# Zero products in tile form and small zero transfers ahead of the first group of a dynamic convolution with a gated output

## The chip, the cores and the metric

The kernel runs on one core of a Trainium2 chip. The metric is the device time of one execution in microseconds (us). TensorE (PE) multiplies matrices, VectorE (DVE) and ScalarE (ACT) work elementwise, GpSimd (POOL) does a few elementwise steps and issues DMAs, and SyncE (SP) only issues DMAs. The DMAs that SP issues form one queue, those of POOL another; both run on the same 16 DMA engines.

## The reference

Eight sequences of 4224 rows and 192 channels. Each row has, for each of 8 heads, 7 weights; a softmax over these 7 weighs the row and the 6 before it. What comes out goes through a causal 5-tap convolution (a sigmoid of it is the gate) and through a product with `w_val`; gate times value is multiplied by `w_out`.

```python
# attention: softmax over the last axis of weight_gen, then
x_unf = x_pad[:, idx, :].reshape(B, S, K, H, group)         # K = 7, H = 8, group = 24
x     = np.einsum('bshk,bskhg->bshg', w, x_unf).reshape(B, S, D)
# gate and output
for k in range(5):
    gate_pre += conv_w[k] * xp[:, k:k + S, :]
out = (1 / (1 + np.exp(-gate_pre))) * (x @ w_val) @ w_out
```

The three weight matrices come as float64 and are turned into float32 on the chip.

## The kernel before

Two sequences make a pair; there are 4 pairs, each cut into 9 groups of 480 rows (the last 384), so 36 groups.

**Softmax.** The class `Softmax` handles a chunk of rows of a pair: the first pair has four chunks (8, 8, 16 and 34 rows to a partition), every later pair two (34 and 32). A chunk is loaded into `wt` by two DMAs on SP, one for each sequence (L262). DVE takes maximum, difference, sum and quotient (L273 to L298), ACT the exponential (L284). ACT then spreads the weights into a banded layout in `zt` (`spread`, L310), twelve rows to a piece, and POOL stores each piece to DRAM in `zd` (`store`, L316).

**Groups.** A group loads its rows of x into `xt` (`load_x`, L391) and the bands into `tb` (`load_t`, L417: sixteen DMAs of 16x4x176 float32 each), all on SP. In `bank` (L439) TensorE multiplies the band by x in tiles of 128x32: 64 products to a group, each of which stands in the trace as two records, so 128 records to a group. ACT copies the four banks out of PSUM (`S`, `B`, `A`; L450 to L457), POOL moves strips between partitions by DMA (L466, L468), ACT and DVE form the gate (L474 to L486), TensorE the value (`val`, L494 to L501) and the output product (`omm`, L522 and L529), ACT copies the result out (L544), and SP stores it (L551). `tb` exists twice (`tb_75` and `tb_76`, used in turn), `xt` three times.

**Ahead of the groups.** DVE zeroes `zero` and the two `zt`; ACT and POOL zero the two `tb`; POOL reorders, loads and converts the weights. `stir(14)` has TensorE form 14 bfloat16 products of 128x128 by 128x368 out of `zero`; nothing reads them.

**Order.** All of it is first entered in a list (`Order.add`: engine, assumed duration, a key, dependencies) and then written out engine by engine by a planner, `Order.run`: at each step it takes the engine that can start earliest, and of the entries open there the one with the smallest key. So an entry added early can change the order of everything behind it. What an engine gets is a fixed sequence, and it works through it in that order; SP too, so that a DMA waiting for its data holds up every DMA behind it. Real waits come from the data alone: a reader of a tile waits for its writer, a writer for earlier readers and writers. Besides, SP's DMAs use eight completion counters in turn, so that a DMA also waits for the eighth before it.

The end of the list of preparations before the change:

```python
    placed = [add("ACT", 0.35, 0.9, f, [conv["v"], wz]) for f in place_weights()]
    add("PE", 2.0, -50, lambda: stir(14), [z0], mode=(0,))
```

Of the kernel before, what the change touches and what calls it, by code (L numbers as in the profile page):

```python
# [7 lines left out]
FP32 = mybir.dt.float32  # L8
U32 = mybir.dt.uint32
I64 = mybir.dt.int64  # L10
BF16 = mybir.dt.bfloat16
# [5 lines left out]
class Order:  # L17
# [13 lines left out]
    def add(self, eng, dur, key, fn, deps=(), mode=None, lag=0.0, bytes=0):  # L31
        o = self.Op()
        o.eng, o.dur, o.key, o.fn, o.mode, o.lag, o.bytes = eng, dur, key, fn, mode, lag, bytes
        o.deps = [d for d in dict.fromkeys(deps) if d is not None]
        o.users, o.ready = [], 0.0
        self.ops.append(o)
        return o
# [47 lines left out]
def tile_dynconv_gated_moe(  # L85
# [9 lines left out]
    nc = tc.nc  # L95
# [5 lines left out]
    P = 128  # L101
    HD = P // 2
    Q = 32
# [18 lines left out]
    PITCH = RUN + CELL // 2  # L122
# [6 lines left out]
    const = ctx.enter_context(tc.tile_pool(name="const", bufs=1))  # L129
    wpool = ctx.enter_context(tc.tile_pool(name="wpool", bufs=2))  # L130
    work = ctx.enter_context(tc.tile_pool(name="work", bufs=2))
    dpool = ctx.enter_context(tc.tile_pool(name="dpool", bufs=1, space=bass.MemoryType.DRAM))
    ps_a = ctx.enter_context(tc.tile_pool(name="ps_a", bufs=3, space=bass.MemoryType.PSUM))
# [9 lines left out]
    wvd = const.tile([P, P], FP32, name="wvd")  # L143
    wvm = const.tile([P, HD], FP32, name="wvm")
    zero = const.tile([P, PITCH], FP32, name="zero")
    NWT = 2 * D + KC
    wf = const.tile([P, 2, NWT], FP32, name="wf")
    un = const.tile([P, 2, NWT], U32, name="un")
    raw_t = const.tile([P, 4 * NWT], FP32, name="raw")
    raw = raw_t.bitcast(U32).rearrange("p (g n t) -> p g n t", g=2, t=2)  # L150
# [14 lines left out]
    add = od.add  # L165
# [52 lines left out]
    def place_weights():  # L218

        units = []  # L220

        def runs(dst, src, q0, q1):

            d = dst.rearrange("p (a c) -> p a c", c=Q)
            return ((d[:, :, 0:C], src[:, C * q0:C * q1].rearrange("p (a c) -> p a c", c=C)),
                    (d[:, :, C:Q], src[:, c6 + HC * q0:c6 + HC * q1].rearrange("p (a c) -> p a c", c=HC)))

        pairs = [*runs(wvm, wf[:, 0, 0:D], 4, NQ)]
        for b in range(2):
            hs = slice(HD * b, HD * b + HD)  # L230
            pairs += runs(wvd[hs, hs], wf[hs, 1, 0:D], 4, NQ)
        pairs += [*runs(wva, wf[:, 0, 0:D], 0, 4), *runs(wvb, wf[:, 1, 0:D], 0, 4)]
        for d, v in pairs:
            units.append(lambda d=d, v=v: nc.scalar.copy(out=d, in_=v))  # L234
        return units
# [129 lines left out]
    rows = {}  # L365
# [184 lines left out]
                          ap=[[2 * D, h], [S * D, 2], [1, 2 * D]])  # L550
            nc.sync.dma_start(out=dst, in_=self.ot[0:h, :, k, :])  # L551

    def stir(n):

        z = zero.bitcast(BF16)
        pa = ps_a.tile([P, 512], FP32, name="pa")
        for _ in range(n):
            nc.tensor.matmul(out=pa[:, 0:2 * PITCH], lhsT=z[:, 0:P], rhs=z, start=True, stop=True)

    def once(eng, dur, key, fn, deps=(), **kw):
        return add(eng, dur, key, fn, deps, **kw)

    z0 = once("DVE", 0.3, -99, lambda: nc.vector.memset(zero, 0.0))
# [4 lines left out]
    front = []  # L570

    def fronts(i):
        for u in range(2):
            nc.gpsimd.dma_start(out=zd[i][u, 0:FRONT, :], in_=zero[0:FRONT, :])

    front = [once("POOL", 1.2, -97.5 + 8 * i, lambda i=i: fronts(i), [z0], lag=2.5, bytes=1) for i in range(2)]
# [17 lines left out]
    conv = {}  # L594
    for name, cs, w, key in (("c", slice(2 * D, NWT), "DVE", 0.3), ("v", slice(0, D), "POOL", 0.5),
                             ("o", slice(D, 2 * D), "POOL", 1.5)):
        a = lw
        for eng, f in convert_weights(cs, "DVE", w):
            dur = 0.2 if name == "c" else 0.6 if eng == "DVE" else 1.5
            a = add(eng, dur, key, lambda f=f, eng=eng: f(engs[eng]), [a])  # L600
        conv[name] = a
    placed = [add("ACT", 0.35, 0.9, f, [conv["v"], wz]) for f in place_weights()]
    add("PE", 2.0, -50, lambda: stir(14), [z0], mode=(0,))

# [11 lines left out]
    for m, gp in enumerate(gr):  # L618
        d = {}
        T.append(d)  # L620
        n, w = gp.n, gp.w
# [11 lines left out]
        last = min(gp.s + NW * gp.step, S)  # L633
# [82 lines left out]
```

## Time and profile before

| | |
|---|---|
| Time, two runs | 642.34 and 643.53 us, median 642.93 |
| Span of the profiled execution, first to last instruction | 638.4 us (4.5 us below the median of the runs) |
| Mean granted TensorE clock | 0.888 |
| Busy: PE, DVE, ACT, POOL | 497.9, 432.8, 343.6, 205.3 us |
| Moved by DMA | 122.19 MB, mean 191 GB/s |

The page has the busy times, the span in 40 slices, the DMA queues, the chain of waits that ended last, and groups of instructions. "PEclk" is the share of full clock that TensorE was granted. The views used below are the timeline (start, duration, engine, line, operation), the table of stretches (busy time of each engine in a stretch, its clock and its DMA share), the chain in order of time, and the table of DMA issues with their time to landing. "SPq" and "POOLq" are the queues of these engines.

### The profile page before, as it was taken

How to read it: one execution, taken by the hardware profiler on the slowest of the kernel's cores; microseconds unless marked ns; L12 is line 12 of the kernel's file. 1: busy time of each engine (PE TensorE's matmuls, PEld its weight loads, DVE VectorE, ACT ScalarE, POOL GpSimd, SP SyncE). 2: the span in 40 equal slices, each digit the busy share in tenths (PEclk: the TensorE clock that was granted, in tenths of full speed). 3: DMA queues.
4: the chain of work that ended last, by engine and by line, in shares of the span. 5: the costliest groups of instructions: out<-in, count | busy, mean ns of one | idle time of the engine just before them, and what ended most of it. 6: DMA issues, size and time to landing. Idle time of an engine off the chain costs nothing.

```text
span 638.4 us, 15889 instructions
## 1 busy us (share of the span) xinstructions
PE 497.9 (78%) x6278; PEld 341.2 (53%) x6278; DVE 432.8 (68%) x488; ACT 343.6 (54%) x533; POOL 205.3 (32%) x380
## 2 busy tenths in 40 slices
PE   2036179859679996997769709999389999999995
PEld 1024156546556665665537506766256667766764
DVE  4646768845867895984765564988656488667780
ACT  6235447635655674764635543586336565665542
POOL 9662132323232332322312230442304422342220
PEclk7567589969898998998888867999789999999999
DMA  6967788878688787687877686786858767777633
GB/s 188 268 128 191 184 230 243 200 193 188 158 225 246 216 211 208 178 256 186 230 181 191 174 200 187 185 201 158 239 122 207 205 173 224 180 193 179 165 81 83
DMA packets 116249, 122.19 MB, mean 191 GB/s; under 512 B 20144, under 2 KB 110348, under 8 KB 113424
## 3 DMA queue, kind: packets, MB, share of 16 engines
q1 hardware_dynamic: 102144, 88.31, 53.3%
q0 software_dynamic: 14032, 32.87, 19.9%
q8 instruction: 50, 0.82, 0.6%
q14 instruction: 23, 0.19, 0.1%
HBM read 63.71 MB, written 51.45 MB: 180 GB/s over the span
## 4 chain that ended last, share of the span: by engine, by line
PE 48%; DMA 26%; SPq 15%; ACT 4%; DVE 3%; issue 3%; POOL 1%; ACTq 0%; DVEq 0%; POOLq 0%
PE pa L439 14%; SPq L417 12%; PE po L522 11%; DMA tb<-zd 11%; PE po L529 6%; PE v L498 6%; DMA wt<-in_weight_gen_dram 5%; DMA zd<-zt 4%; PE v L501 4%; PE v L496 4%; PE v L494 3%; DMA out_dram<-ot 3%; SPq L391 2%; ACT zt L310 1%; DMA A<-S 1%
## 5 line engine op out<-in xcount | busy, mean ns | idle before, releaser
L439 PE MATMUL pa<-tb,xt 128*32 128x122 f32 (+3 forms) x4608 | 156.0, 293 | 119.8 <-DMA tb<-zd 111.6
L439 PEld LDWEIGHTS pa<-tb,xt 128*32 128x32 f32 (+3 forms) x4608 | 141.5, 120 | 134.8 <-issue 64.6
L482 DVE SCALAR_TENSOR_TENSOR aA<-A,wf,aA 128x960 f32<-128x960 f32 (+1 forms) x144 | 171.1, 1188 | 25.1 <-ACT aA L474 23.2
L468 POOL DMA_DIRECT2D B<-S x144 | 74.2, 522 | 281.4 <-ACT B L453 272.4
L482 DVE SCALAR_TENSOR_TENSOR aB<-B,wf,aB 128x480 f32<-128x480 f32 (+1 forms) x144 | 101.1, 702 | 75.8 <-ACT aB L477 74.4
L522 PE MATMUL po<-wf,aA 128*120 128x192 f32 (+1 forms) x576 | 116.4, 347 | 8.3 <-ACT ot L544 3.9
L544 ACT COPY ot<-po 120x768 f32<-120x768 f32 (+1 forms) x72 | 57.8, 803 | 114.3 <-PE po L529 70.3
L522 PEld LDWEIGHTS po<-wf,aA 128*120 128x120 f32 (+1 forms) x576 | 94.3, 191 | 40.3 <-issue 24.8
L466 POOL DMA_DIRECT2D A<-S x144 | 74.6, 524 | 49.3 <-ACT A L450 23.2
L457 ACT COPY S<-pa 64x484 f32<-64x484 f32 (+1 forms) x72 | 39.7, 552 | 67.7 <-PE pa L439 67.2
L529 PE MATMUL po<-wf,aB 64*120 64x192 f32 (+1 forms) x576 | 69.8, 361 | 5.2 <-DVE aB L509 3.5
L498 PE MATMUL v<-A,wva 128*128 128x480 f32 (+1 forms) x144 | 62.7, 558 | 1.4 <-ACT wva L234 1.4
L529 PEld LDWEIGHTS po<-wf,aB 64*120 64x120 f32 (+1 forms) x576 | 47.3, 190 | 21.5 <-issue 14.3
L507 DVE TENSOR_TENSOR aA<-v,aA 128x960 f32<-128x960 f32 (+1 forms) x36 | 40.7, 1130 | 23.0 <-ACT aA L486 15.7
L474 ACT ACTIVATE aA<-A,wf 128x960 f32<-128x960 f32 (+1 forms) x36 | 38.8, 1077 | 24.0 <-DMA A<-S 23.7
L316 POOL DMA_DIRECT2D zd<-zt x50 | 26.8, 540 | 72.3 <-ACT zt L310 59.7
L450 ACT COPY A<-pa 128x484 f32<-128x484 f32 (+1 forms) x72 | 39.8, 553 | 12.2 <-PE pa L439 11.1
L498 PEld LDWEIGHTS v<-A,wva 128*128 128x128 f32 x144 | 27.3, 190 | 31.1 <-issue 26.8
L310 ACT COPY zt<-wt 128x192 f32<-128x192 f32 (+3 forms) x100 | 39.0, 463 | 7.8 <-DVE wt L298 3.9
L486 ACT ACTIVATE aA<-aA 128x960 f32<-128x960 f32 (+1 forms) x36 | 35.3, 980 | 8.3 <-DVE aA L482 8.2
L509 DVE TENSOR_TENSOR aB<-v,aB 128x480 f32<-128x480 f32 (+1 forms) x36 | 23.1, 641 | 24.3 <-ACT aB L486 19.0
L494 PE MATMUL v<-A,wvm 128*64 128x480 f32 (+1 forms) x144 | 38.1, 609 | 0.0
(55 smaller groups left out, 371.3 us busy)
## 6 DMA issues: line engine op xcount, KB each, us to landing
tb<-zd SPq DMA_DIRECT2D x560, 44.0 KB
out_dram<-ot SPq DMA_DIRECT2D x64, 360.0 KB
xt<-in_x_dram SPq DMA_DIRECT2D x56, 384.0 KB
zd<-zt POOLq DMA_DIRECT2D x30, 552.0 KB, 6.8
wt<-in_weight_gen_dram SPq DMA_DIRECT2D x8, 560.0 KB
A<-S POOLq DMA_DIRECT2D x128, 30.2 KB, 3.7
zd<-zt POOLq DMA_DIRECT2D x10, 368.0 KB, 8.0
zd<-zt POOLq DMA_DIRECT2D x8, 460.0 KB, 9.1
```

What stands on the lines that cost most here:

```text
L310: nc.scalar.copy(out=dst, in_=src)
L417: nc.sync.dma_start(out=t[lo:lo + n, u * NW + w0:u * NW + w1, c0:c0 + RUN], in_=src)
L439: nc.tensor.matmul(out=pa[Q * c:Q * c + Q, at:at + n], lhsT=self.xb[0:k, u * NW + j, C * h:C * h + Q], rhs=self.t[0:k, u * NW + j, PAD // ...
L466: nc.gpsimd.dma_start(out=self.A[q:q + n, :, 0:w], in_=self.S[p:p + n, :, 0:w])
L468: nc.gpsimd.dma_start(out=self.B[HD * u + q:HD * u + q + n, 0:w], in_=self.S[p:p + n, u, 0:w])
L482: nc.vector.scalar_tensor_tensor(out=a, in0=src, scalar=cw[:, g, j:j + 1], in1=a, op0=ALU.mult, op1=ALU.add)
L494: nc.tensor.matmul(out=v2[HD * u:HD * u + HD, 0:n], lhsT=wvm, rhs=A[:, u], start=True, stop=False, tile_position=(0, HD * u))
L498: nc.tensor.matmul(out=v01[:, u, 0:n], lhsT=wva, rhs=A[:, u], start=True, stop=False)
L507: nc.vector.tensor_tensor(out=self.aA, in0=self.v01[:, :, 0:n], in1=self.aA, op=ALU.mult)
L522: nc.tensor.matmul(out=po[0:h // 2, u, D * t:D * t + D], lhsT=gA[:, u, k, t], rhs=woa, start=first and t == 0, stop=not first, skip_group_ ...
L529: nc.tensor.matmul(out=po[0:h // 2, u, D * t:D * t + D], lhsT=gB[hs, k, t], rhs=wob[hs], start=first and t == 0, stop=not first, skip_grou ...
L544: nc.scalar.copy(out=self.ot[0:h, :, k, :], in_=self.po[0:h, :, 0:2 * D])
```

## The change

`stir` takes a kind now and forms float32 products in tiles: kinds 5 and 6 form 64 products of 128x32 by 128x122 each, kinds 2, 3 and 4 form 160 products of 64x32 by 64x58 each. The kinds differ in how the moving operand is read (`t` pairs with a stride, or single columns with a stride) and, for kind 4, in the PSUM bank that is written. Seven of them are entered one behind the other: 6, 5, 6, 2, 3, 4, 5. They read a new zero tile `scr` of 128x2048, which DVE writes. Nothing reads what they form.

`lay` is new: four entries on SP, 37 DMAs that carry zeros from `scr` to a new DRAM buffer `zs`, from there to a new tile `scr2`, and from `scr` to `scr2`. Nothing reads `scr2`.

```diff
+    scr = const.tile([P, 2048], FP32, name="scr")
+    big = scr
+    scr2 = const.tile([P, 2048], FP32, name="scr2")
+    zs = dpool.tile([P * 8, 184], FP32, name="zs")
...
-    def stir(n):
-        z = zero.bitcast(BF16)
-        pa = ps_a.tile([P, 512], FP32, name="pa")
-        for _ in range(n):
-            nc.tensor.matmul(out=pa[:, 0:2 * PITCH], lhsT=z[:, 0:P], rhs=z, start=True, stop=True)
+    def stir(kind):
+        w = zero[:, 0:PITCH]
+        bk = [ps_a.tile([P, 512], FP32, name="pa") for _ in range(2)]
...
+        elif kind < 4:
+            for i in range(20):
+                for u in range(2):
+                    for c in range(4):
+                        ps = slice(HD * u, HD * u + HD)
+                        mv = (big[ps, 0:464].rearrange("p (a h t) -> p a h t", h=8, t=2)[:, :, c, :] if kind == 2 else
+                              big[ps, 0:464].rearrange("p (a h) -> p a h", h=8)[:, :, c])
+                        nc.tensor.matmul(out=bk[u][Q * c:Q * c + Q, 64 * (i % 8):64 * (i % 8) + 58], lhsT=w[ps, Q:2 * Q],
+                                         rhs=mv, start=True, stop=True, tile_position=(HD * u, Q * c))
+        elif kind == 4:
...
+        else:
+            for i in range(16):
+                for c in range(4):
+                    mv = (big[:, 0:976].rearrange("p (a h t) -> p a h t", h=8, t=2)[:, :, c, :] if kind == 5 else
+                          big[:, 0:976].rearrange("p (a h) -> p a h", h=8)[:, :, c])
+                    nc.tensor.matmul(out=bk[0][Q * c:Q * c + Q, 128 * (i % 4):128 * (i % 4) + 122], lhsT=w[:, Q:2 * Q],
+                                     rhs=mv, start=True, stop=True, tile_position=(0, Q * c))
+
+    def lay(part):
+        if part == 0:
+            nc.sync.dma_start(out=zs.rearrange("(p r) n -> p (r n)", r=8), in_=scr[:, 0:8 * 184])
+            for n in (56, 112):
+                dst = bass.AP(tensor=zs.tensor, offset=zs.offset, ap=[[184 * 8, P], [184, 8], [1, n]])
+                nc.sync.dma_start(out=dst, in_=scr[:, 0:8 * n].rearrange("p (c n) -> p c n", n=n))
+        elif part == 1:
+            for n, q, c in ((56, P, 16), (112, P, 8)):
+                src = bass.AP(tensor=zs.tensor, offset=zs.offset, ap=[[n, q], [P * n, c], [1, n]])
+                nc.sync.dma_start(out=scr2[0:q, 0:c * n].rearrange("p (c n) -> p c n", n=n), in_=src)
+        else:
+            for r in range(16):
+                src = scr[0:HD, 56 * r:56 * r + 56]
+                if part == 2:
+                    nc.sync.dma_start(out=scr2[r:r + HD + 1:HD, 0:1792].rearrange("p (c n) -> p c n", n=56), in_=src)
+                else:
+                    nc.sync.dma_start(out=scr2[r + 16:r + 17, 0:1792].rearrange("p (c n) -> p c n", n=56), in_=scr[0:Q, 56 * r:56 * r + 56])
...
-    add("PE", 2.0, -50, lambda: stir(14), [z0], mode=(0,))
+    b0 = once("DVE", 1.0, -98.5, lambda: nc.vector.memset(scr, 0.0))
+    last = None
+    for k in (6, 5, 6, 2, 3, 4, 5):
+        last = add("PE", 3.0, -50, lambda k=k: stir(k), [z0, b0, last], mode=(0,))
+    for k in range(4):
+        add("SP", 4.0, -88.5 + 0.1 * k, lambda k=k: lay(k), [b0, *front])
```

How the DMAs stand on SP after the early loads of x, before the change (`wt` is a softmax chunk, `tb` a band; the last figures are the shape, `x16` means sixteen in a row):

```order
L391 DMA xt_81<-in_x_dram 128x3x192
L262 DMA wt<-in_weight_gen_dram 64x1232
L262 DMA wt<-in_weight_gen_dram 64x2240
L262 DMA wt<-in_weight_gen_dram 64x1232
L417 DMA tb_75<-zd_79 16x4x176 x16
L262 DMA wt<-in_weight_gen_dram 64x2240
L417 DMA tb_76<-zd_79 16x4x176 x16
```

and after it, where line numbers are 4 higher up to the old `stir` and 67 higher behind it, and `scr_90` is the tile `scr2`:

```order
L395 DMA xt_81<-in_x_dram 128x3x192
L607 DMA zs<-scr 128x1472
L610 DMA zs<-scr 1024x1x56
L610 DMA zs<-scr 1024x1x112
L614 DMA scr_90<-zs 128x16x56
L614 DMA scr_90<-zs 128x8x112
L619 DMA scr_90<-scr 2x32x56 x16
L621 DMA scr_90<-scr 1x32x56 x16
L266 DMA wt<-in_weight_gen_dram 64x1232
L421 DMA tb_75<-zd_79 16x4x176 x7
L266 DMA wt<-in_weight_gen_dram 64x1232
L421 DMA tb_75<-zd_79 16x4x176 x9
```

All 37 new DMAs stand between the last early load of x and the load of the first pair's third softmax chunk (64x1232). Each of the first five writes or reads what the one before it wrote, and the sixth writes over what the fifth wrote. The two loads of the third chunk, which stood two apart, now have seven loads of `tb` between them, and the two of the fourth chunk (64x2240) stand behind the sixteen of `tb_75` and behind nine of `tb_76`.

On TensorE the last bfloat16 products of zeros stood right ahead of the first group's products of `tb_75`:

```order
L558 MATMUL pa<-zero 128x368
L558 LDWEIGHTS zero
L558 MATMUL pa<-zero 128x368
L439 MATMUL pa<-tb_75,xt_81 32x122 x12
L439 MATMUL pa<-tb_75,xt_81 32x118 x4
```

After the change the sequence begins with 736 products in tiles (the figure behind x counts products; the trace has two records for each):

```order
L600 MATMUL pa<-scr,zero 32x122 x192
L584 MATMUL pa<-scr,zero 32x58 x320
L593 MATMUL pa<-scr,zero 32x58 x160
L600 MATMUL pa<-scr,zero 32x122 x64
L443 MATMUL pa<-tb_75,xt_81 32x122 x12
```

The 14 bfloat16 products are gone, and the first group's product of `tb_75` follows the last product of zeros. The order of the entries behind the start is planned anew too, so that the places of output stores among the loads of `tb` differ in the later groups.

More of the change, by code (lines that the diff above doesn't have):

```diff
@@ L551, in store, with rounds @@
             nc.sync.dma_start(out=dst, in_=self.ot[0:h, :, k, :])
-    def stir(n):
-        z = zero.bitcast(BF16)
-        pa = ps_a.tile([P, 512], FP32, name="pa")
-        for _ in range(n):
-            nc.tensor.matmul(out=pa[:, 0:2 * PITCH], lhsT=z[:, 0:P], rhs=z, start=True, stop=True)
+    def stir(kind):
+        w = zero[:, 0:PITCH]
+        bk = [ps_a.tile([P, 512], FP32, name="pa") for _ in range(2)]
+        def rounds(n, rows, cols, cells):
+            h = P // rows
+            for i in range(n):
+                for u in range(h):
+                    for c in range(4):
+                        ps = slice(rows * u, rows * u + rows)
+                        mv = w[ps, 0:2 * cells * 8].rearrange("p (a h t) -> p a h t", h=8, t=2)[:, :, c, :] if cols else \
+                            w[ps, 0:2 * cells * 8].rearrange("p (a h) -> p a h", h=8)[:, :, c]
+                        nc.tensor.matmul(out=bk[(u + i) % 2 if h == 2 else u % 2][Q * c:Q * c + Q, 64 * (i % 4) + 32 * (u // 2):][:, 0:2 * cells],
+                                         lhsT=w[ps, Q:2 * Q], rhs=mv, start=True, stop=True,
+                                         tile_position=(rows * u, Q * c))
+        if kind < 2:
+            rounds(20, P, kind == 0, 11)
+        elif kind < 4:
[8 more added lines that the diff above has]
+        elif kind == 4:
+            for i in range(20):
+                for u in range(2):
+                    for c in range(4):
+                        ps = slice(HD * u, HD * u + HD)
+                        mv = big[ps, 0:464].rearrange("p (a h t) -> p a h t", h=8, t=2)[:, :, c, :]
+                        d = bk[(c // 2 + u) % 2]
+                        nc.tensor.matmul(out=d[Q * c:Q * c + Q, 64 * (i % 8):64 * (i % 8) + 58], lhsT=w[ps, Q:2 * Q],
+                                         rhs=mv, start=True, stop=True, tile_position=(HD * u, Q * c))
+        else:
+            for i in range(16):
+                for c in range(4):
+                    mv = (big[:, 0:976].rearrange("p (a h t) -> p a h t", h=8, t=2)[:, :, c, :] if kind == 5 else
+                          big[:, 0:976].rearrange("p (a h) -> p a h", h=8)[:, :, c])
+                    nc.tensor.matmul(out=bk[0][Q * c:Q * c + Q, 128 * (i % 4):128 * (i % 4) + 122], lhsT=w[:, Q:2 * Q],
+                                     rhs=mv, start=True, stop=True, tile_position=(0, Q * c))
```

## The prediction

> **What bounds the kernel now.** I read the table of stretches first, to see which stage is thin. Its columns are the stretch, the busy time of PE, PEld, DVE, ACT and POOL, the granted clock, the DMA share and GB/s.
>
> ```profile
> core 0: us, PE busy (x) PEld busy (x) DVE busy (x) ACT busy (x) POOL busy (x), PEclk, DMA share, GB/s
> 16.00:32.00 16.00, 0.00 (x0) 0.00 (x0) 10.44 (x23) 3.37 (x9) 10.09 (x14) 0.50 0.94 270
> 32.00:48.00 16.00, 5.03 (x128) 4.65 (x128) 7.97 (x11) 5.11 (x13) 10.17 (x13) 0.70 0.62 126
> 64.00:80.00 16.00, 2.60 (x48) 2.35 (x52) 12.23 (x15) 7.38 (x13) 2.63 (x5) 0.55 0.77 181
> 200.00:300.00 100.00, 90.19 (x1119) 61.89 (x1119) 76.59 (x83) 59.75 (x89) 29.14 (x57) 0.97 0.78 209
> 300.00:400.00 100.00, 72.29 (x856) 49.26 (x858) 61.66 (x69) 48.47 (x77) 24.16 (x47) 0.81 0.76 194
> ```
>
> PE has nothing to do up to 32 us and little up to 80; later it is busy 72 to 90 us in 100. So the start is a chain of latencies, and what lengthens it moves the whole rest, which is dense. The chain of waits in order of time (start, length, what) shows who holds the start:
>
> ```profile
> 4.25 8.36 DMA wt<-in_weight_gen_dram
> ...
> 24.46 9.16 DMA wt<-in_weight_gen_dram
> ...
> 38.31 5.56 DMA tb<-zd
> ...
> 47.27 3.01 DMA tb<-zd
> 50.37 2.14 PE pa L439 x34
> 52.99 1.73 ACT zt L310 x4
> 55.56 8.92 DMA zd<-zt
> ```
>
> Softmax chunks and bands, all loaded by SP. SP's own timeline at the place of the change (start, length of the stretch, issues):
>
> ```profile
> 14.97 2.54 SPq L391 DMA_DIRECT2D xt<-in_x_dram  x6
> 20.93 4.57 SPq L262 DMA_DIRECT2D wt<-in_weight_gen_dram  x3
> 26.91 10.79 SPq L417 DMA_DIRECT2D tb<-zd  x16
> 37.75 0.47 SPq L262 DMA_DIRECT2D wt<-in_weight_gen_dram  x1
> 38.31 9.85 SPq L417 DMA_DIRECT2D tb<-zd  x16
> ```
>
> SP is free from 17.51 to 20.93 (it waits there for a `wt` buffer) and from 25.50 to 26.91; from then to 48.16 it only issues. The other engines' rows, from the timeline:
>
> ```profile
> 1.46 1.90 DVE L567 MEMSET zt<- 128x2208 f32 x1 [0.41 <-issue]
> 12.71 0.97 DVE L273 TENSOR_REDUCE mx<-wt 128x112 f32<-128x784 f32 x1 [7.05 <-DMA wt<-in_weight_gen_dram]
> 33.65 0.80 DVE L273 TENSOR_REDUCE mx<-wt 128x88 f32<-128x616 f32 x1 [4.53 <-DMA wt<-in_weight_gen_dram]
> 38.98 5.03 PE L439 MATMUL pa<-tb,xt 128*32 128x122 f32 x128 [34.03 <-DMA tb<-zd]
> 50.37 5.24 PE L439 MATMUL pa<-tb,xt 128*32 128x122 f32 x96 [6.36 <-DMA tb<-zd]
> 52.53 0.56 ACT L457 COPY S<-pa 64x484 f32<-64x484 f32 x1 [6.80 <-PE pa L439]
> 77.40 5.48 PE L439 MATMUL pa<-tb,xt 128*32 128x122 f32 x96 [13.98 <-DMA tb<-zd]
> 97.19 0.92 PE L529 MATMUL po<-wf,aB 64*120 64x192 f32 x8
> 98.04 3.75 PE L439 MATMUL pa<-tb,xt 128*32 128x122 f32 x128
> ```
>
> The node that counts is group 1's start at 50.37: ACT's copy of its first bank at 52.53 stands ahead of the spread of the third chunk, its stores land at 64.5, and only then come the bands of group 2.
>
> **The change, part by part.** *DVE* gets a memset of 128x2048: 1.90 x 2048/2208 = 1.76, with the gap of 0.41 some 2.2 us. DVE stood idle for 7.05 us until 12.71, which hides it; the price is nothing, and 2.2 us if that wait were gone.
>
> *The 14 bfloat16 products* went beside idle time; nothing is won.
>
> *The zero products.* 64 float32 products were 128 records: 5.03 us at the low clock of 38.98, 3.75 us at 98.04 where the clock was full, so 29 to 39 ns a record. Kinds 5 and 6 are 512 records, 15 to 20 us. Kinds 2 to 4 are 960 records of a form the trace does not have. Its bounds are the same 29 ns, and the row at 97.19, the one with 64-row tiles and a short stretch: 0.92 us for 8 records of 192 columns, 115 ns, which is three times as many columns. The nearer row is that of the 32-column tiles, and 58 columns are half of its 122; I take 29 to 39 ns, 28 to 37 us. With a start at 3.5 us TensorE ends its zeros at 47 to 61 us. Group 0 cannot start before its bands have come, which is later than that, as the next term says: cost nothing. Nor does a warm array bring anything: group 0 would be done 1.3 us sooner, but group 1 waits for its own bands.
>
> *The 37 DMAs on SP* are the term that counts. SP reaches them at 17.51 and passes the third chunk's loads only behind them. First the five that wait for each other. The prices come from the table of DMA issues (KB each, us to landing) and the row of SP's queue:
>
> ```profile
> zd<-zt POOLq DMA_DIRECT2D x30, 552.0 KB, 6.8
> raw<-wd POOLq DMA_DIRECT2D x2, 192.0 KB, 6.2
> raw<-cd POOLq DMA_DIRECT2D x1, 5.0 KB, 3.8
> zd<-zero POOLq DMA_DIRECT2D x4, 7.2 KB, 2.6
> q1 hardware_dynamic: 102144, 88.31, 53.3%
> ```
>
> From below: a small transfer lands in 2.6 us, and the five carry 736, 224, 448, 448 and 448 KB, 2.36 MB, which at the 270 GB/s of the stretch from 16 to 32 are 8.7 us: 5 x 2.6 + 8.7 = 21.7 us. From above: the queue's mean packet takes 0.533 x 638.4 x 16 / 102144 = 53 ns; the four with short pieces have 1024, 1024, 2048 and 1024 of them, on each of 16 engines 64, 64, 128 and 64, so 3.4, 3.4, 6.8 and 3.4 us, and the first 736 KB at 270 GB/s 2.8: with five times 2.6 that is 32.8 us. The pieces are 224 and 448 bytes where the mean packet has 865, so I take a value near the lower end, 23 us. The Trainium skill ("DMA: Bandwidth & Descriptors", Specifications) gives 512 bytes as the least transfer for full rate and speaks of read-modify-write below it; by that the upper end would be the better guess and the sum some 10 us larger. No packet of the trace shows it apart from others.
>
> Then 32 small ones. SP's issue took 0.47 us by itself (37.75) and 10.79/16 = 0.67 us in the stretch that also waited for earlier loads: 15.0 to 21.6 us; with idle queues the lower, 15. So SP is through at 17.5 + 23 + 15 = 55.5 us, with ends of 54 and 72.
>
> Behind it stand the same four chunk loads and 32 bands as before, in another mixture. Before they took 48.16 - 20.93 = 27.2 us, of which 1.4 was the wait at 25.50 for `zd`, which will long be there, and some waits inside the first three: the bands 10.79 + 9.85, four loads at 0.47 to 0.5, 22.6 us in all. Group 1 started 2.2 us after the last band (50.37 - 48.16). So it starts at 55.5 + 22.6 + 2.2 = 80.3 instead of 50.37: +29.9 us. If every issue took 0.47, 36 of them would take 16.9, and it would be 74.6, +24.2. Group 0 gets its bands at 55.5 + 0.9 + 12.1 (38.98 - 26.91) = 68.5, behind the end of the zeros at 47 to 61.
>
> Is the third chunk ready then? Its second load comes 5.7 us behind SP's return and lands at the 9.16 us of the chain at some 70.4; before, it landed at 33.65 and 19.3 us later its spread began, of which 6 were spent behind the fourth chunk's load, which now stands behind it on DVE. So it is ready at some 84, about when group 1's first bank is copied (80.3 + 2.2 = 82.5). From there the chain is the one of before, shifted by 30 us. Nothing takes it back: DVE, ACT and POOL have done the weights meanwhile, but these were not in the chain.
>
> The profiled span was 638.4 and the median 642.93; I add the difference to both alike: 642.93 + 29.9 = 672.8, rounded to **673 us**.
>
> **The rivals.** *The short transfers run on two engines.* Sixteen of them write 2 partitions each. If one is carried by 2 engines, these have 32 pieces each, at 53 ns 1.7 us for one transfer instead of 0.47 for its issue: 16 x 1.2 = 20 us more, **693 us**. The trace cannot tell, as it shows queues and no engines; for the cheap side speak the half-size pieces. The Trainium skill says just this ("DMA: Bandwidth & Descriptors", Why a DMA increments its semaphore by 16 and not by 1): a transfer uses the largest number of engines up to 16 that divides both outer dimensions. I give it 0.13.
>
> *The 64x32 products do not run beside each other.* At 115 ns a record the 960 take 110 us, the zeros end at 3.5 + 20 + 110 = 134, group 0 waits for them, and group 1 starts at 139: +88, **731 us**. It decides from 54 ns a record (75 us less 3.5 and 20, over 960). Against it: four column tiles at 29 ns for 122 columns. 0.04.
>
> *The new order gives it back: not slower.* SP is held by output stores that wait for ACT while bands stand behind them:
>
> ```profile
> SPq L551 <- ACT ot L544: 40.6, 11, 6.5
> ...
> SPq L417 <- DMA xt<-in_x_dram: 18.0, 17, 2.6
> ```
>
> Eleven waits, 40.6 us, up to 6.5 each. The whole later order is planned anew, so some of them may go; 18 us would go if the stretch from 300 to 400 (72.29 us of PE work) ran like the one from 200 to 300 (90.19). With the shift at its lower 23 us that leaves +5, **648 us**; beyond 36 us regained it would be faster by 2%. It decides from 17 us regained. For it: PE waits are large there. Against it: a new order can as well add such waits. 0.13 for not slower by over 2%, 0.04 for faster.
>
> **How the numbers follow.** Forecast 673 with 0.66 of the chance, two engines 0.13, products apart 0.04, given back 0.13 within 2% and 0.04 below. 2% is 12.9 us, about what a measurement can tell from no change. So faster 0.04, same 0.13, slower 0.83. Range: the cheapest SP term, 54.2 with issues of 0.47, gives +23 and 666; with part of the 18 us of a new order 652. The dearest, 72 + 24.8, gives 97, +46.5 and 689; with two engines on top of the middle 693, to 695. So 652 to 695.
>
> **What would show it.** In the changed kernel's timeline: SP's zero loads from 17.5 to some 55, of which the first five have gaps of 2.5 to 6 us between them; the third chunk's load right behind; group 0 at some 68 and group 1 at some 80; PE's zeros over by 61. Wrong it is if SP is through by 40 us, if group 1 starts before 63, or if the end moves by 10 us less or more than group 1's start, which would put the cause into the later order.

## The result and the profile after

The changed kernel takes 679.36 us (two runs, 677.81 and 680.90), against 642.93 before: the medians differ by 36.4 us, and the ratio is 1.058 with a 95% interval of 1.0495 to 1.0668, which is +37 us (+32 to +43). It is slower, as forecast, and inside the stated range, 6 us above the forecast of 673. The profiled span grew by 40.7 us, from 638.4 to 679.1. Here and below, a ratio leaves out executions that took over 1.5% more than the fastest of their kernel, and the microseconds given with it are the ratio applied to the time before, which can lie some 4 us from the difference of the medians.

The timeline of SP in the changed kernel at the place of the change (start, length of the stretch, line, issues):

```profile
15.02 2.55 SPq L395 DMA_DIRECT2D xt<-in_x_dram  x6
17.67 0.43 SPq L607 DMA_DIRECT2D zs<-scr  x1
26.56 5.99 SPq L610 DMA_DIRECT2D zs<-scr  x2
37.17 5.15 SPq L614 DMA_DIRECT2D scr<-zs  x2
45.72 8.91 SPq L619 DMA_DIRECT2D scr<-scr  x16
54.68 10.09 SPq L621 DMA_DIRECT2D scr<-scr  x16
64.89 0.52 SPq L266 DMA_DIRECT2D wt<-in_weight_gen_dram  x1
65.51 3.34 SPq L421 DMA_DIRECT2D tb<-zd  x7
...
82.25 3.39 SPq L421 DMA_DIRECT2D tb<-zd  x7
```

The third chunk's load, which went out at 20.93, now goes out at 64.89. In between stand the five transfers that wait for each other (17.67 to 45.72, with holes) and the 32 small ones (to 64.77, without a hole). The chain in order of time shows the five landings one behind the other:

```profile
17.67 8.88 DMA zs<-scr
26.56 5.37 DMA zs<-scr
31.99 5.16 DMA zs<-scr
37.17 4.76 DMA scr<-zs
41.95 3.76 DMA scr<-zs
```

TensorE's and ACT's timelines, the rows that answer to those of before:

```profile
3.25 18.09 PE L600 MATMUL pa<-scr,zero 128*32 128x122 f32 x384 [3.25 <-DVE scr L665]
21.27 1.14 PE L584 MATMUL pa<-scr,zero 64*32 64x58 f32 x95
...
52.13 2.87 PE L600 MATMUL pa<-scr,zero 128*32 128x122 f32 x97 [1.17 <-issue]
76.73 5.91 PE L443 MATMUL pa<-tb,xt 128*32 128x122 f32 x128 [21.73 <-DMA tb<-zd]
91.51 4.57 PE L443 MATMUL pa<-tb,xt 128*32 128x122 f32 x96 [8.87 <-DMA tb<-zd]
93.80 0.56 ACT L461 COPY S<-pa 64x484 f32<-64x484 f32 x1 [10.55 <-PE pa L443]
94.26 2.50 ACT L314 COPY zt<-wt 128x192 f32<-128x192 f32 x8
```

The zeros end at 55.0 us, 21.7 us before group 0 has its bands. Group 1 starts at 91.51 instead of 50.37 (+41.1), the third chunk's spread at 94.26 instead of 52.99 (+41.3). The span grew by 40.7. So in these two executions all of it is there before the third group, and nothing is given back or lost in the 580 us behind it.

### The profile page after: what moved, and what is told of

It reads as the page before. It is cut to its first block, busy times and chain, and to the rows that moved or that the text cites. A ratio compares the mean times of both kernels' runs of the same rounds, so it can differ in the third digit from the quotient of the medians.

```text
span 679.1 us, 18853 instructions
## 1 busy us (share of the span) xinstructions
PE 528.6 (78%) x7736; PEld 366.7 (54%) x7736; DVE 434.4 (64%) x489; ACT 343.8 (51%) x533; POOL 204.5 (30%) x380
## 3 DMA queue, kind: packets, MB, share of 16 engines
q0 software_dynamic: 14032, 32.87, 19.1%
## 4 chain that ended last, share of the span: by engine, by line
PE 51%; DMA 24%; SPq 13%; ACT 5%; issue 4%; DVE 1%; POOL 0%; ACTq 0%; DVEq 0%
PE pa L443 15%; PE po L526 13%; SPq L421 8%; DMA out_dram<-ot 7%; PE po L533 7%; PE v L502 6%; DMA tb<-zd 5%; PE v L500 4%; DMA wt<-in_weight_gen_dram 4%; PE v L505 4%; PE v L498 4%; DMA zs<-scr 3%; DMA zd<-zt 2%; ACT zt L314 2%; SPq L621 1%
## 5 line engine op out<-in xcount | busy, mean ns | idle before, releaser
L443 PE MATMUL pa<-tb,xt 128*32 128x122 f32 (+3 forms) x4608 | 150.8, 285 | 88.4 <-DMA tb<-zd 72.2
L443 PEld LDWEIGHTS pa<-tb,xt 128*32 128x32 f32 (+3 forms) x4608 | 135.6, 116 | 105.4 <-issue 88.0
L486 DVE SCALAR_TENSOR_TENSOR aA<-A,wf,aA 128x960 f32<-128x960 f32 (+1 forms) x144 | 170.9, 1187 | 18.4 <-ACT aA L478 14.4
L526 PE MATMUL po<-wf,aA 128*120 128x192 f32 (+1 forms) x576 | 119.6, 353 | 12.7 <-ACT ot L548 8.4
L526 PEld LDWEIGHTS po<-wf,aA 128*120 128x120 f32 (+1 forms) x576 | 96.9, 195 | 44.4 <-issue 21.7
L533 PE MATMUL po<-wf,aB 64*120 64x192 f32 (+1 forms) x576 | 69.6, 362 | 24.2 <-DVE aB L513 23.3
L511 DVE TENSOR_TENSOR aA<-v,aA 128x960 f32<-128x960 f32 (+1 forms) x36 | 40.8, 1132 | 23.6 <-PE v L505 12.5
L478 ACT ACTIVATE aA<-A,wf 128x960 f32<-128x960 f32 (+1 forms) x36 | 38.8, 1077 | 24.9 <-DMA A<-S 22.2
L277 DVE TENSOR_REDUCE mx<-wt 128x160 f32<-128x1120 f32 (+3 forms) x18 | 21.5, 1197 | 45.9 <-DMA wt<-in_weight_gen_dram 45.9
```

The costliest lines, as they stand in the source:

```text
L443: nc.tensor.matmul(out=pa[Q * c:Q * c + Q, at:at + n], lhsT=self.xb[0:k, u * NW + j, C * h:C * h + Q], rhs=self.t[0:k, u * NW + j, PAD // ...
L486: nc.vector.scalar_tensor_tensor(out=a, in0=src, scalar=cw[:, g, j:j + 1], in1=a, op0=ALU.mult, op1=ALU.add)
L511: nc.vector.tensor_tensor(out=self.aA, in0=self.v01[:, :, 0:n], in1=self.aA, op=ALU.mult)
L526: nc.tensor.matmul(out=po[0:h // 2, u, D * t:D * t + D], lhsT=gA[:, u, k, t], rhs=woa, start=first and t == 0, stop=not first, skip_group_ ...
L533: nc.tensor.matmul(out=po[0:h // 2, u, D * t:D * t + D], lhsT=gB[hs, k, t], rhs=wob[hs], start=first and t == 0, stop=not first, skip_grou ...
```

## The experiments

The theory: SP's queue is held for as long as it stands and issues; the third chunk's spread moves by that, and the end moves with the spread. The rivals: the planner's new order makes part of it; the zero products do; the traffic of the transfers does, wherever they stand.

The names: in the kernels whose label begins with o, the rest is in the order of the kernel before, DVE writes the zero tile `scr` right behind `zero`, and the transfers, where there are any, are put by hand in front of the third chunk's load; "n_none" has the changed kernel's order. The cuts of code leave out lines; they show what differs from the changed kernel or, where a transfer is altered, from o_lay.

**The transfers alone (o_lay).**

```diff
+        def first(u):
+            if p == 0 and R == 16 and u == 0:
+                for k in range(4):
+                    lay(k)
-            ld.append(add("SP", 0.5, ..., lambda u=u: s.load(u), ...))
+            ld.append(add("SP", 0.5, ..., lambda u=u: first(u) or s.load(u), ...))
```

> The kernel before in its own order, with its 14 bfloat16 products, and the 37 zero transfers put in front of the load of the third softmax chunk without the planner's knowledge. Theory (SP's queue is the price): in the changed kernel SP was held from 17.67 to 64.8 us; behind that stand the loads and bands that took some 25 us from there to group 1's start, so group 1 starts at some 90 us instead of 50.4, and the time is 643 + 39 = 682 us. Rival (the new order makes a good part of the 36 us): clearly less, some 655 to 670. Rival (the zero products make it): 643.

677.28 us, ratio 1.058 (1.050 to 1.066), +37 us. ACT's timeline has the start of the spread:

```profile
90.03 2.52 ACT L314 COPY zt<-wt 128x192 f32<-128x192 f32 x8
```

That is 37.0 us later than before. The transfers by themselves make the whole loss, as far as the intervals tell.

**The zero products alone (o_zeros)**: the same kernel with `stir` of the seven kinds and without `lay`.

> The kernel before in its own order, with the 736 zero products in place of the 14 bfloat16 products and without the 37 transfers. Theory: the zeros end at 55 us as in the changed kernel; here the bands of group 0 are there at 39 and those of group 1 at 50, so TensorE's zeros become the bound of the start: group 0 from 55, group 1 right behind at 59 instead of 50.4, and 643 + 9 = 652 us. Rival (a warmer array brings something, group 1 catches up): 643 or less. Rival (zero products cost nothing anywhere): 643.

657.99 us, ratio 1.022 (1.014 to 1.031), +14 us (+9 to +20), where +9 was expected. Its timeline on TensorE and ACT:

```profile
56.24 2.88 PE L605 MATMUL pa<-scr,zero 128*32 128x122 f32 x97 [0.41 <-issue]
58.89 1.05 PE L448 MATMUL pa<-tb,xt 128*32 128x122 f32 x28
60.16 5.84 PE L448 MATMUL pa<-tb,xt 124*32 124x118 f32 x196 [0.22 <-issue]
...
65.20 2.46 ACT L314 COPY zt<-wt 128x192 f32<-128x192 f32 x8
```

The zeros end at 59, not 55, groups 0 and 1 come right behind, and the spread starts 12.2 us later than before. So the products are not free in themselves: they are hidden in the changed kernel because the transfers hold the bands back for longer.

**Both, in the order of before (o_both).**

> Both parts of the change, but in the order of the kernel before (the planner does not know of them). Theory: as with the transfers alone, since the zeros end long before the bands come: some 682 us, group 1 at 90. If the two add up, 691. If the new order of the changed kernel cost time by itself, this one is faster than its 679.

678.70 us, ratio 1.060 (1.053 to 1.066); the spread starts at 92.14. The two parts don't add up: the longer covers the shorter.

**The changed kernel's order without its work (n_none)**: `lay` and `stir` stand in the planner's list and issue nothing.

```diff
-        add("SP", 4.0, -88.5 + 0.1 * k, lambda k=k: lay(k), [b0, *front])
+        add("SP", 4.0, -88.5 + 0.1 * k, lambda k=k: None, [b0, *front])
```

(the seven PE entries likewise, but that one of them issues the 14 old products).

> The planner is told of both parts as in the changed kernel, so that everything behind the start has the changed kernel's order, but the 37 transfers and the zero products are not issued (the 14 bfloat16 products are; the zero tile is still written). Theory (the order is neutral): 643 within 1%. Rival (the order gives or takes): beyond 1%, and by as much the changed kernel's 36 us are not the transfers'.

640.87 us, ratio 0.998 (0.995 to 1.002). The new order is neutral, and that rival falls. The spread starts 2.5 us later than before all the same:

```profile
55.49 2.50 ACT L314 COPY zt<-wt 128x192 f32<-128x192 f32 x8
```

So the time follows the spread's start only to within a few microseconds. Against n_none, the kernel in its own order, the change's spread starts 38.8 us later, and the medians differ by 38.5.

**Five transfers, and 32 (o_five, o_small)**: as o_lay with `range(2)`, and with `(2, 3)`, instead of `range(4)`.

> The order of the kernel before, its bfloat16 products, and only the first five of the 37 transfers, those that wait for each other. Theory: SP is held from 17.7 for 28 us, to 45.7, group 1 starts at some 71 instead of 50.4 and the time is 643 + 20 = 663 us. Rival (not SP's time but the bytes moved count; the five carry nearly all of them): as with all 37.

> The order of the kernel before, its bfloat16 products, and only the 32 small transfers. Theory: SP is held from 17.7 for their 19 us of issue, to 37, group 1 starts at some 62 and the time is 643 + 11 = 654 us. Rival (transfers into two partitions run on two engines and hold what is queued behind them): the third chunk's load lands late though SP is through, group 1 well after 62. Rival (bytes count, and these carry few): 643.

o_five: 659.41 us, ratio 1.026 (1.019 to 1.033), +17 us, where +20 was expected; the spread starts at 68.14, +15.2. o_small: 662.35 us, ratio 1.026 (1.020 to 1.032), +17 us; the spread at 71.43, +18.4, where some +11 was expected. The 32 carry 0.34 MB, a seventh of what the five carry, and cost as much, so bytes are not the price. Nor do they hold what is queued behind them beyond their issue: the first bands go out at 45.46 instead of 26.91, 18.6 us later, which is all of the spread's shift. They cost more than expected since their issue takes longer right behind the loads of x. SP's issues of the first sixteen in o_small and in the changed kernel, where they come 28 us later and the DMA engines are nearly idle (share 0.11 to 0.14 from 46 to 54 us; least, median and longest duration in ns):

```profile
L631 SPq DMA_DIRECT2D scr<-scr x16: 504/528/2937, 17.6 to 32.8; - x16
```

```profile
L619 SPq DMA_DIRECT2D scr<-scr x16: 504/505/632, 45.7 to 54.1; - x16
```

**The same 37 without the chain (o_unchained).**

```diff
-                for k in range(4):
+                for k in (0, 2, 3, 1):
                     lay(k)
-            for n in (56, 112):
-                dst = bass.AP(tensor=zs.tensor, ...)
+            for n, z in ((56, zsb), (112, zsc)):
+                dst = bass.AP(tensor=z.tensor, ...)
```

(and the first of the two loads goes to a tile of its own, and `scr` and `scr2` are no wider than is used).

> The order of the kernel before, its bfloat16 products, and all 37 transfers with the same shapes and bytes, but to buffers of their own and in another sequence (the three stores, the 32 small ones, the two loads), so that none but the last waits for another one's landing by its data. Theory (the price is the time that SP stands and issues): SP is through at 41 to 45 instead of 65, group 1 starts at 66 to 70, the time is 643 + 16 to 20 = 659 to 663 us. Rival (the traffic of the transfers is the price): as with all 37 in their chain.

668.00 us, ratio 1.039 (1.034 to 1.044), +25 us. That is 9 us by the medians and 12 by the ratios less than with the chain, at the same bytes, so the rival that puts the whole price on the traffic falls; but it is more than the 16 to 20 us that were expected. SP's timeline and the durations of its issues tell why:

```profile
17.61 0.42 SPq L620 DMA_DIRECT2D zs<-scr  x1
18.08 0.62 SPq L623 DMA_DIRECT2D zsb<-scr  x1
18.74 1.18 SPq L623 DMA_DIRECT2D zsc<-scr  x1
19.97 17.73 SPq L632 DMA_DIRECT2D scr<-scr  x16
37.74 10.11 SPq L634 DMA_DIRECT2D scr<-scr  x16
...
49.78 2.16 SPq L267 DMA_DIRECT2D wt<-in_weight_gen_dram  x3
```

```profile
L632 SPq DMA_DIRECT2D scr<-scr x16: 504/505/7949, 20.0 to 37.2; - x16
```

Without the holes the stores queue up behind the loads of x, and one small issue took 7.95 us while the stretches of 22 to 30 us had the DMA engines full:

```profile
22.00:26.00 4.00, 0.00 (x0) 0.00 (x0) 0.68 (x5) 0.33 (x2) 1.05 (x2) 1.00 1.03 367
26.00:30.00 4.00, 0.00 (x0) 0.00 (x0) 3.33 (x10) 0.00 (x0) 1.81 (x3) 1.00 1.05 350
```

(the last two figures are the DMA share and GB/s). So SP was through at 49.7 instead of 41 to 45, and the spread began at 79.69, +26.7. Traffic does count, then, where it lengthens the issue.

**An outer dimension of 2 (o_two)**: the second and third of the five carry the same 896 pieces of 224 bytes, with 896 and with 2 outer rows.

```diff
-            for n in (56, 112):
-                dst = bass.AP(tensor=zs.tensor, offset=zs.offset, ap=[[184 * 8, P], [184, 8], [1, n]])
+            for outer in ([[184 * 8, 112], [184, 8]], [[184 * 520, 2], [184, 448]]):
+                dst = bass.AP(tensor=zs.tensor, offset=zs.offset, ap=[*outer, [1, 56]])
```

> The order of the kernel before with the five chained transfers, but the second and third now carry the same 896 pieces of 224 bytes, once to an outer dimension of 896 rows and once to one of 2. Each is waited for by the next. Theory (pieces cost some 17 ns as the changed kernel's rows say, and all transfers spread over the 16 engines alike): both land in 4 to 6 us. Rival of the prediction (an outer dimension of 2 runs on two engines): the second takes 448 pieces an engine, 7.6 us for them alone, so 9 to 11 us to land, where the first takes 4 to 6.

The chain of waits in order of time; the second and third row are the two:

```profile
17.60 8.44 DMA zs<-scr
26.06 5.22 DMA zs<-scr
31.35 10.11 DMA zs<-scr
41.47 3.71 DMA scr<-zs
```

5.22 against 10.11 us, as the rival expected. No view shows engines, so that it is two of them is inferred from the time. With 448 pieces to an engine the 4.9 us more are spread over 392 pieces more (448 less 56): 12 ns a piece. The single execution took 659.26 us, and its spread started at 74.74, +21.8.

**Group 1's first bands on ACT's queue (f_act, f_new).** Does the end also follow when the start moves forward? ACT stands idle from 24 to 37 us in the kernel before, so the sixteen loads of `tb` for group 1 were issued there, in the old order (f_act) and in that of n_none (f_new).

```diff
-                nc.sync.dma_start(out=t[lo:lo + n, ...], in_=src)
+                (eng or nc.sync).dma_start(out=t[lo:lo + n, ...], in_=src)
...
+        def after_store(u):
+            if p == 0 and r0 == 512 and u == 1:
+                for j in range(-(-(gr[1].step + PAD) // G)):
+                    for v in range(2):
+                        gr[1].load_t(j, v, nc.scalar)
```

> The kernel before without any of the change; the sixteen loads of group 1's first bands are issued by ACT instead of SP, right behind the store of the second chunk. Theory (the end follows group 1's start): group 1 starts right behind group 0 at some 44 to 46 instead of 50.4, but the third chunk's spread is only ready at 50 instead of 53, so the time falls by 3 us, to 640. Rival (other waits take the place): no change, or slower because ACT is held while it waits for the store.

640.06 us, ratio 0.997 (0.994 to 1.001): no difference that can be told. Group 1's first bank was copied 3 us earlier, but the spread was not; DVE's and ACT's timelines:

```profile
46.07 1.32 DVE L273 TENSOR_REDUCE mx<-wt 128x160 f32<-128x1120 f32 x1 [9.43 <-DMA wt<-in_weight_gen_dram]
49.47 0.55 ACT L464 COPY S<-pa 64x484 f32<-64x484 f32 x1
52.51 2.44 ACT L310 COPY zt<-wt 128x192 f32<-128x192 f32 x8 [2.48 <-DVE wt L298]
```

DVE stood 9.4 us at the fourth chunk's load with the third chunk unfinished behind it. In the order of n_none it finishes the third chunk first:

> None of the change's transfers and zero products, but the changed kernel's order (measured neutral: ratio 0.998), in which DVE finishes the third chunk before it takes up the fourth; and group 1's sixteen first bands issued by ACT. When they were moved in the old order, group 1 came right behind group 0 but the third chunk's spread began at 52.5 us as before (52.99), because DVE stood 9.4 us at the fourth chunk's load. Theory (the end follows the start of that spread): here the chunk is ready at some 48, the spread begins 4 to 6 us earlier than in the kernel before and the time is 637 to 639 us, ratio 0.990 to 0.994. Rival (what is won at the start is lost to other waits): ratio 1.0 within its interval.

The median of six executions is 635.70 us, 5.4 less than the 641.10 of the kernel before in the same series; by the ratio, 0.985 (0.979 to 0.991), it is 10 us less (6 to 13). ACT's timeline:

```profile
48.88 0.57 ACT L468 COPY S<-pa 64x484 f32<-64x484 f32 x1 [1.36 <-PE pa L450]
49.96 2.48 ACT L314 COPY zt<-wt 128x192 f32<-128x192 f32 x8 [0.51 <-DVE wt L302]
```

The spread begins 3.0 us earlier than before and 5.5 earlier than in n_none (55.49), whose time was that of the kernel before. So the time fell where the spread started earlier; by how much stays open. The profiled execution, 638.38 us, has a span 1.8 us shorter than that of before; the six lie between 629.41 and 641.50, those of before between 636.27 and 647.46, and none of those near 629 was profiled.

The kernels with parts of the change, beside each other. The last three columns are differences from the kernel before; the change and n_none have the new order.

| | third chunk's spread starts, us | its shift | span of the same execution | time, us (95%) |
|---|---|---|---|---|
| before | 52.99 | | | |
| new order alone (n_none) | 55.49 | +2.5 | -2.1 | -1 (-3 to 1) |
| zero products alone | 65.20 | +12.2 | +19.8 | +14 (9 to 20) |
| five transfers | 68.14 | +15.2 | +23.6 | +17 (12 to 21) |
| 32 transfers | 71.43 | +18.4 | +23.3 | +17 (13 to 21) |
| five, one on an outer dimension of 2 | 74.74 | +21.8 | +19.1 | +18 (one execution) |
| 37, no chain | 79.69 | +26.7 | +30.7 | +25 (22 to 28) |
| 37 | 90.03 | +37.0 | +38.6 | +37 (32 to 42) |
| 37 and products, old order | 92.14 | +39.2 | +43.0 | +38 (34 to 42) |
| the change | 94.26 | +41.3 | +40.7 | +37 (32 to 43) |

In each row with an interval and with zero products or transfers, the spread's shift lies within the interval of the time. In a single execution the span can differ from the shift by up to 8 us; where that difference arises behind the start stays open.

## Why the prediction was right

*DVE's memset* cost nothing, as argued: TensorE's zeros start at 3.25, and DVE's next work still waited for its load.

*The zero products* were to end at 47 to 61 us and be hidden; they ended at 55.0 and were hidden. The end came out by luck, for neither price was right in its reason. The 512 records of 128x32 took 23.8 us where 15 to 20 were taken: the first 128 of kind 5 went at 28 ns a record, the 256 of kind 6, for which the same price was taken, at 56. The 960 of 64x32 took 28.05 us (21.27 to 49.32), 29 ns each, the lower end, but that is an average of 11 to 17 ns a record and of pauses (the last section has both). That they cost nothing was right only beside the transfers; the 12 us that they cost alone were not named as the price if that cover were gone.

*The five chained transfers* were the term that was mis-sized most: 23 us taken, 28.05 measured (17.67 to 45.72), inside the bounds of 21.7 and 32.8. The first alone took 8.88, where 5.4 stood in the sum of the upper bound; the DMA engines were full (share 1.03 from 21 to 29 us) with what was under way on SP's and POOL's queues. I went near the lower end because of the short pieces; the middle of the bounds would have been right.

*The 32 small ones*: 15 taken at 0.47 an issue, 19.05 measured. No row had their form. Sixteen took 0.50 us each and the other sixteen 0.59 (with 0.04 between issues), and what the form costs was to be had from no row of the kernel before.

*What stands behind them*: 24.8 taken, 26.6 measured (64.89 to 91.51). The issues took 20.8 instead of 22.6, and group 1 came 5.9 us behind the last band instead of 2.2. The chain has the last band's landing:

```profile
85.22 6.27 DMA tb<-zd
```

In the kernel before it took 3.01. The longer wait goes with the new order, which has the fourth chunk's second load seven bands before the last (81.74): in n_none, too, group 1 came 5.8 us behind the last band, in o_lay 2.4.

Together 17.67 + 28.05 + 19.17 + 26.62 = 91.51 against the 80.3 of the prediction, 11 us more. The mechanism, that a later start of group 1 and of the spread moves the end by about as much, holds in every row with zero products or transfers; the table says how closely. The profiled spans follow it (+40.7), while the median of the runs moved by 36.4; the interval holds both. That the time was missed by 6 us only, and group 1's start by 11, is therefore scatter between executions and not merit.

*The third chunk* was forecast to be ready at some 84, about when group 1's bank is copied; it was ready at 83.6, with ACT's copy at 93.80, so it had 10 us to spare. That the 84 was met is luck: SP came back 9.4 us later than forecast, but the second load landed in 4.2 us where 9.16 was taken (69.69 to 73.91), and from there the chunk took 9.7 us instead of 13.3.

*The rival of two engines* had the right mechanism, which the Trainium skill states ("DMA: Bandwidth & Descriptors", Why a DMA increments its semaphore by 16 and not by 1); the runs agree with it, 10.11 against 5.22 us. It was the price that was wrong: at 53 ns a piece the 32 pieces of an engine would have outlasted the issue; at the 12 ns of o_two, measured on stores to DRAM, they would take 0.4 us (an estimate), less than the 0.50 of the issue, and stay hidden. *The rival of products that don't run beside each other* falls: 29 ns a record, and 54 was its threshold. *The rival of the new order* falls with n_none at 0.998. Its two thresholds went by different shifts, 17 us by the middle one of 29.9 and 36 by the lower one of 23; by the middle the second would be 43.

The other sentence of the Trainium skill that the prediction weighed, that pieces below 512 bytes are written by read-modify-write ("DMA: Bandwidth & Descriptors", Specifications), is not told apart by any run here: no run varied the size of the pieces alone.

## What to carry to other kernels

Work that feeds nothing is not free if it stands in an in-order queue that the start of the kernel goes through: what counts is the time until the next load behind it goes out, landings that it waits for included. Where a start is a chain of latencies and the rest is dense, find the one instruction through which the start passes to the rest (here the third chunk's spread); its shift can be read in one profile and gives the change of the time, here to within the intervals of the runs, which are some 3 to 6 us to either side. And two covers can hide each other: price each part with the other gone.

## What the runs showed of the hardware

- The issue of one DMA on SP depended on its form and on the traffic: 0.50 us for 2 rows of 32 pieces, 0.59 for one row of 32 pieces, though that has half the pieces, and up to 7.95 us where the DMA engines were full.
- What the moving operand's columns looked like doubled the time of a float32 product. Kinds 5 and 6 have the same shape; kind 5 reads pairs of neighbouring columns with a stride, kind 6 single columns with a stride. In the changed kernel the first 128 records (kind 6) took 7.12 us, the next 128 (kind 5) 3.62, the next (kind 6) 7.28, with a granted clock of 1.00 throughout: 56, 28 and 57 ns a record. In o_zeros and o_both it was 56, 32 or 33, and 57.
- Dense float32 products in small tiles came in bursts, with TensorE idle between them and nothing to wait for that the profile names. The changed kernel's timeline:

```profile
23.84 1.44 PE L584 MATMUL pa<-scr,zero 64*32 64x58 f32 x128 [1.43 <-issue]
28.94 2.16 PE L584 MATMUL pa<-scr,zero 64*32 64x58 f32 x128 [3.65 <-issue]
32.66 2.00 PE L584 MATMUL pa<-scr,zero 64*32 64x58 f32 x128 [1.56 <-issue]
```

Within a burst a record took 11 to 17 ns, over all 29. The queue that loads instructions moved 12 packets more than before, 0.20 MB more, while TensorE's products and weight loads grew by 2 x 1458. The rows of before and of the changed kernel (packets, MB, share):

```profile
q8 instruction: 50, 0.82, 0.6%
```

```profile
q8 instruction: 62, 1.02, 0.6%
```

It is 62 in o_zeros and o_both too, and 50 in o_lay, so the packets come with the products. The added bytes are some 69 an instruction, and a burst is 128 records and as many weight loads, 256 instructions, about one packet of the added 0.20/12 MB. The traces have the times of the packets, 16384 bytes each. In the changed kernel packets were through at 22.54, 27.68, 31.40 and 35.86 us, and bursts began at 23.84, 28.94, 32.66 and 37.22. The zero products pause eight times for over 0.8 us in each of the three kernels that have them; each time, 256 instructions run from one pause to the next, and TensorE goes on 1.2 to 1.6 us after the end of such a packet. So in this stretch TensorE waited for its instructions; no run removed that wait.
